# Delta attention, routed experts and a dense layer: five small moves in the first stage

## The chip, the cores and the metric

One core of a Trainium2 chip runs the whole program. The metric is device time in microseconds (us), from three executions of each kernel. Views of the profile come from one further execution, recorded by the hardware profiler.

## The reference

```python
# 1. delta-rule attention, 4 batches x 8 heads, 768 steps, head size 48
k_n = k / (norm(k) + 1e-6)
for t in range(768):
    y[t]  = q[t] @ state
    v_old = k_n[t] @ state
    state = state + beta[t] * outer(k_n[t], v[t] - v_old)
x = y reshaped to 3072 tokens x 384
# 2. router and experts: 8 experts, the best two for each token
logits = x @ w_gate + log1p(exp(x @ w_noise)) * noise
for each token and its best two experts: out += weight * relu(x @ w1[e]) @ w2[e]
# 3. dense layer
h = out @ w_in ; out = (h * clip(h + 3, 0, 6) / 6) @ w_out
```

## The kernel before, in words

The attention works on 24 tiles of 128 tokens (two batches of 64 steps each, all heads). Within a tile the recurrence is written as a triangular system. Its matrix is inverted for four tiles at once, a group, by some 60 VectorE instructions: `inverse_ops(g)`, 1 of 6 groups. They begin with `head`, which transposes the Gram blocks `gd` into `A`, clears `T`, and end with `tail`, which transposes `T` into `Xc` and `Yc`.

The main loop takes two tiles per turn, n = 0, 2, ..., 18. The order of TensorE in a turn is written out by hand: some warming matmuls on zeros (`warm`, L480), `merge1`(n), `ks`(n), the Gram products of tile n+8 (`gram`, L183, into one PSUM tile `gm` that ScalarE evicts at L187 to L205), `merge2`(n), `ks`(n+1), `merge1`(n+1), the router's transposes of tile n-2 (`transposes`, L839), `solve`(n), `merge2`(n+1), transposes of n-1, the router's logits (L852), `update`, `solve`(n+1), `output`, the Gram products of n+9, `update` and `output` of n+1. `merge1` and `solve` of tile n need `Xc` of its group, so a group's inverse must be through when the turn n = 4, 8, 12, 16 or the tail after the loop begins. The tail takes tiles 20 to 23 and starts with `ks`, transposes and `merge1`(20). ScalarE does nearly every eviction of PSUM there.

The instructions of an inverse wait in a list (`pend`) with a cost each; after every step of TensorE `run` lets out as many as the step's time covers. The router works on four tiles at once (`route`, started in the turns n = 4, 8, 12, 16): `scale` (exp and ln on ScalarE, L879 and L880, each with a table load), `noisy` (23 small VectorE instructions, woven one by one between those of the inverse), `count` (sums of the choices, on GpSimd for tiles 0 to 11, on VectorE from tile 12), `rank` (matmuls into a PSUM tile `rk`, read by VectorE at L929 among the woven instructions) and `place` (which queues the scatters of token numbers on GpSimd, `move`). `step` starts the next of these when the last one's woven instructions are out. The tiles `wp`, `tpx`, `lg`, `rk`, `rkt` and half the outputs `y` take turns in two PSUM buffers with the tag `tp`.

In turn n = 18, `reserve` sums the counts of tiles 0 to 15 on TensorE (`rkt`, L818) to find how much of the first expert's block of 512 slots is left over, and shifts that expert's base by it. SyncE issues all loads and stores of the attention in order; the store of an output tile (L834) stands ahead of the next load of queries and keys (`load_qk`, L161).

After the attention come the experts (L1196 and L1219, from 326.6 us of the span), then the dense layer (L1525 and L1557, from 807 us).

Of the kernel before, what the change touches and what calls it, by code (L numbers as in the profile page):

```python
# [16 lines left out]
NH = 8  # L17
CH = 64
P0 = 10
W0 = (3, 6)  # L20
PB = 10
M1_AT = {4: (1, 4, 7), 5: (2, 5), 6: (1, 4)}
W1_AT = {4: (5,), 5: (0,), 6: (0,)}
# [18 lines left out]
EXP = 8  # L42
# [47 lines left out]
def emit_attention(ctx, tc, qk, k, v, beta, const, rt, moe):  # L90
# [156 lines left out]

    big = pr.tile([128, 1024], F32, name="big")
    TT = pr.tile([128, 16, 16], F32, name="TT")

    def blocks(t):
        return t.rearrange("p (s r) -> p s r", s=2)[:, :, 0:512].rearrange("p s (t k) -> p s t k", k=32)[:, :, :, 0:16]

    def inverse_ops(g):
        ops = []
        Af = pr.tile([128, 1056], F32, tag="A", name="A", bufs=1)
        Tf = pr.tile([128, 1056], F32, tag="T", name="T", bufs=1)
        A, T = [t[:, 0:1024].rearrange("p (t i) -> p t i", i=32) for t in (Af, Tf)]
        Ab, Tb = blocks(Af), blocks(Tf)
        scratch = pr.tile([128, 256], F32, tag="tmp", name="tmp", bufs=1)  # L260
# [11 lines left out]

        def head():
            if g:
                nc.gpsimd.memset(Tf[:, 0:1024], 0.0)
            V.transpose(out=A, in_=gd[g].rearrange("p j t -> p t j"))
            V.tensor_copy(out=n2, in_=Af[:, 0:1024:33])
            if g == 0:
                nc.scalar.sqrt(s, n2)
# [228 lines left out]
    def step(drain=False):  # L508
        if drain:
            while stages or micro[0]:  # L510
                while micro[0]:
                    pend.pop(0)[1]()
                if stages:
                    weave(stages.pop(0)() or [])
        elif stages and not micro[0]:
            weave(stages.pop(0)() or [])
            run(0.0)

    def straight(k):
# [94 lines left out]
    for n in range(0, NT - 4, 2):  # L614
        a = n + LA
        four = n % 4 == 0
        pc[0] = a
        if not four and a // 4 + 1 < NG:
            load_beta(a // 4 + 1)
        for i in range(2):  # L620
            live(load_v, n + 4 + i)
            if n + 4 < NT:
                live(load_k, n + 2 + i)
        for i in range(2):
            if n + 2 + i > 3:
                live(v_norm, n + 2 + i)
        if n == NT - 6:
            moe.snapshot(pk, ps2)
            rt.reserve()
        if n:  # L630
            warm(W0[four])
            live(merge1, n)
            live(prep, n)
            live(ks, n)
            live(gram, a)
            live(prep, n + 1)
            live(merge2, n)
            flush(2)
            live(ks, n + 1)
            live(merge1, n + 1)  # L640
            rt.transposes(n - 2, xs.pop(n - 2))
            if n == NT - 6:
                straight(2)
            else:
                step()
            live(solve, n)
            live(merge2, n + 1)
            flush()
            rt.transposes(n - 1, xs.pop(n - 1))
            rt.logits(n - 2)  # L650
        else:
            live(solve, n)
            live(gram, a)
            flush()
        step()
        live(update, n)
        live(solve, n + 1)
        if n:
            rt.logits(n - 1)
            if four:  # L660
                step(True)
                stages += rt.route(n - 4, 4)
                step()
        live(output, n)
        live(load_qk, a + 2)
        if n == NT - 8:
            run(1.0)
            straight(2)
        else:
            step()  # L670
        live(gram, a + 1)
        live(update, n + 1)
        flush(2)
        live(output, n + 1)
        if n == NT - 6:
            while rt.moves:
                rt.moves.pop(0)[1]()
                if not rt.moves:
                    moe.snap_load()
        flush()  # L680
        live(load_qk, a + 3)
        if n != NT - 8:
            step()
        if not four:
            run(0.0, True)
            if n == NT - 10:
                step()
            if n // 4 + 2 < NG:
                pend += inverse_ops(n // 4 + 2)
                run(2.3)  # L690
# [32 lines left out]
    merge2(n + 3)  # L723
    ks(n + 2)
    ks(n + 3)
    stages.pop(0)()
    micros = stages.pop(0)()

# [39 lines left out]
class Router:  # L768
# [87 lines left out]
    def route(self, n, w):  # L856
# [19 lines left out]
        def scale():  # L876
            while self.defer_act:
                self.defer_act.pop(0)()
            nc.scalar.activation(out=e, in_=z, func=ACTF.Exp)  # L879
            nc.scalar.activation(out=l, in_=e, func=ACTF.Ln, bias=1.0)  # L880

        def noisy():
# [35 lines left out]
        def rank():  # L918
            rk = self.ps.tile([128, 4, 128], F32, tag="tp", name="rk", bufs=2)
            out = rk[:, 0, 0:w * EXP]  # L920
            nc.tensor.matmul(out, lhsT=self.ones, rhs=self.base.unsqueeze(1).to_broadcast([128, w, EXP]),
                             start=True, stop=False)
            for j in range(w - 1):
                nc.tensor.matmul(out[:, (j + 1) * EXP:], lhsT=self.ones,
                                 rhs=cnt[:, j].unsqueeze(1).to_broadcast([128, w - 1 - j, EXP]),
                                 start=False, stop=False)
            nc.tensor.matmul(out, lhsT=self.upper, rhs=cnt.rearrange("p j e -> p (j e)"), start=False, stop=True)
            return [
                lambda: V.tensor_tensor(out=pos, in0=out.rearrange("p (j e) -> p j e", e=EXP),  # L929
                                        in1=self.ebase.unsqueeze(1).to_broadcast([128, w, EXP]), op=ALU.add),  # L930
                lambda: V.tensor_tensor(out=oh, in0=oh, in1=pos.unsqueeze(2).to_broadcast([128, w, 2, EXP]),
                                        op=ALU.mult),
                lambda: V.tensor_reduce(out=sf, in_=oh, axis=AX.X, op=ALU.add),
                lambda: V.tensor_copy(out=self.slots[:, n:n + w], in_=sf),
            ]
# [13 lines left out]
        def place():  # L949
            self.moves += [(j, lambda j=j, k=k: move(j, k)) for j in range(n, n + w) for k in range(2)]  # L950

        return scale, noisy, count, rank, place


def overflow_table(tc, rt, kp):
# [123 lines left out]
class Moe1:  # L1079
# [81 lines left out]
    def emit(self, ctx, wd, m2, x_last):  # L1161
# [106 lines left out]
        def tail(f):  # L1268
            if f == 0:
                first[0]()  # L1270
                micro.extend(first[1]())
                rt.transposes(NT - 1, x_last)
                rt.logits(NT - 2)
            elif f == 1:
                some(99)
                first[2]()
                rt.logits(NT - 1)
                final[0]()
            elif f == 2:
                put_pairs(*first[3:])  # L1280
                micro.extend(final[1]())
            elif f == 3:
                some(99)
                final[2]()
            elif f == 4:
                put_pairs(*final[3:])
                rt.total()
                load_ids()
            elif f == 5:
                for q in rt.defer_act + rt.defer_dve:  # L1290
                    q()
                rt.defer_act, rt.defer_dve = [], []
                wd.load()
                self.load(1, 1)
                wd.load()
# [372 lines left out]
```

## Time and profile before

| | us |
|---|---|
| median of 3 executions | 1204.99 |
| lowest and highest | 1200.16, 1214.01 |
| the profiled execution | 1217.92 |
| its span, first to last instruction | 1216.2 |
| TensorE busy in the span | 1145.9 (94%) |
| VectorE, ScalarE, GpSimd busy | 676.5, 510.5, 304.5 |

Times in the views are microseconds from the start of the span. "Idle before" is the time in which an engine stood still ahead of an instruction, with what ended it behind the arrow. The granted clock is TensorE's, as a share of 2.4 GHz.

### The profile page before, as it was taken

What the parts mean: (1) busy time and instruction counts of PE and PEld (TensorE: products, weight loads), DVE (VectorE), ACT (ScalarE), POOL (GpSimd) and SP (SyncE); (2) the same over time, 40 slices, a digit from 0 to 9 for tenths busy, and PEclk for the clock granted to TensorE, in tenths of its full rate; (3) what the DMA queues carried; (4) which work ended last, traced back from release to release, by engine and by line L of the source; (5) the groups of instructions that cost most, each with busy time, mean ns of one, the idle gap of its engine ahead of it and who ended that gap; (6) DMA issues with size and microseconds to landing.
All of it is one profiled execution on the core that took longest, in us unless ns stands there. A gap on an engine that the chain in (4) does not pass through costs nothing. (4 is left out here: it accounts for less than half of the span.)

```text
span 1216.2 us, 25655 instructions
## 1 busy us (share of the span) xinstructions
PE 1145.9 (94%) x10572; PEld 1052.3 (87%) x10587; DVE 676.5 (56%) x1568; ACT 510.5 (42%) x1053; POOL 304.5 (25%) x375
## 2 busy tenths in 40 slices
PE   8888888868789999999999999989999999999998
PEld 5677777757678999999999999978989898999988
DVE  7998677683454858575656644435161524425150
ACT  5667666633542423232333333346151524334240
POOL 4643254564334231414141311124000000000000
PEclk9887797956799999999999999999999999999999
DMA  7652242323216644444453320442102020100000
GB/s 193 144 133 68 67 109 54 80 41 79 94 40 217 229 164 143 151 162 153 126 170 135 126 91 32 145 156 78 51 3 72 7 66 13 49 30 6 22 1 27
DMA packets 56220, 113.35 MB, mean 93 GB/s; under 512 B 9368, under 2 KB 37221, under 8 KB 55334
## 3 DMA queue, kind: packets, MB, share of 16 engines
q1 hardware_dynamic: 47142, 90.32, 25.0%
q0 software_dynamic: 8448, 19.70, 4.9%
q10 hardware_dynamic: 512, 1.67, 0.6%
q8 instruction: 84, 1.38, 0.5%
q14 instruction: 34, 0.28, 0.1%
HBM read 83.74 MB, written 26.08 MB: 90 GB/s over the span
## 5 line engine op out<-in xcount | busy, mean ns | idle before, releaser
L1219 PE MATMUL yp<-w2h,ht 128*128 128x384 f32 x832 | 221.1, 340 | 0.0
L1219 PE MATMUL yp<-w2l,ht 128*128 128x384 f32 x448 | 150.2, 335 | 0.0
L1219 PEld LDWEIGHTS yp<-w2h,ht 128*128 128x128 f32 x832 | 148.4, 188 | 0.3
L1009 POOL DMA_INDIRECT y<-ys,idp x56 | 64.9, 1159 | 301.2 <-DVE ys L1228 222.6
L1196 PE MATMUL hp<-xth,w1h 128*128 128x416 f32 (+2 forms) x384 | 137.1, 357 | 1.2 <-DVE xtl L1138 1.2
L1196 PE MATMUL hp<-xtl,w1h 128*128 128x416 f32 (+2 forms) x384 | 135.9, 354 | 0.0
L1196 PE MATMUL hp<-xth,w1l 128*128 128x416 f32 (+2 forms) x384 | 135.8, 354 | 0.0
L1557 PE MATMUL yp<-woh,gh 128*128 128x384 f32 x384 | 130.4, 340 | 0.0
L1557 PE MATMUL yp<-woh,gl 128*128 128x384 f32 x384 | 129.1, 336 | 0.0
L1557 PE MATMUL yp<-wol,gh 128*128 128x384 f32 x384 | 129.1, 336 | 0.0
L1199 ACT ACTIVATE ht<-hp 128x416 fp32r<-128x416 f32 (+2 forms) x128 | 66.4, 519 | 134.6 <-PE hp L1196 120.3
L1202 DVE SCALAR_TENSOR_TENSOR ht<-hp,ht 128x352 fp32r<-128x352 f32 (+3 forms) x192 | 79.2, 441 | 64.8 <-ACT ht L1199 63.7
L1525 PE MATMUL hp<-xh,wih 128*128 128x512 f32 x288 | 112.8, 392 | 2.6 <-DVE three L1511 2.6
L1525 PE MATMUL hp<-xh,wil 128*128 128x512 f32 x288 | 112.9, 392 | 0.0
L1525 PE MATMUL hp<-xl,wih 128*128 128x512 f32 x288 | 112.7, 391 | 0.0
L1534 DVE TENSOR_TENSOR gl<-r,gh 128x512 fp32r<-128x512 f32 x96 | 66.5, 693 | 79.2 <-ACT gh L1533 79.2
L1528 ACT ACTIVATE r<-hp,three 128x512 f32<-128x512 f32 x96 | 66.2, 690 | 88.9 <-PE hp L1525 81.3
L1530 DVE SCALAR_TENSOR_TENSOR r<-r,hp 128x512 f32<-128x512 f32 x96 | 65.3, 681 | 53.1 <-ACT r L1528 53.1
L1219 PEld LDWEIGHTS yp<-w2l,ht 128*128 128x128 f32 x448 | 84.2, 188 | 0.0
L1196 PEld LDWEIGHTS hp<-xth,w1h 128*128 128x128 f32 x384 | 72.7, 189 | 3.6 <-DVE xtl L1138 1.6
L1564 ACT ACTIVATE os<-yp 128x384 f32<-128x384 f32 x23 | 11.3, 492 | 153.7 <-PE yp L1557 153.7
L1196 PEld LDWEIGHTS hp<-xth,w1l 128*128 128x128 f32 x384 | 72.8, 190 | 2.0
(227 smaller groups left out, 2217.9 us busy)
## 6 DMA issues: line engine op xcount, KB each, us to landing
r<-in_moe_w_dram SPq DMA_DIRECT2D x16, 768.0 KB
r<-in_moe_w_dram SPq DMA_DIRECT2D x21, 512.0 KB
yg<-y SPq DMA_DIRECT2D x24, 384.0 KB
wd_r<-in_moe_w_in_dram SPq DMA_DIRECT2D x6, 1024.0 KB
wd_r<-in_moe_w_out_dram SPq DMA_DIRECT2D x8, 768.0 KB
mq<-in_qk_dram SPq DMA_DIRECT2D x28, 192.0 KB
v<-in_v_dram SPq DMA_DIRECT2D x24, 192.0 KB
xd<-x SPq DMA_DIRECT2D x24, 192.0 KB
```

The costliest lines, as they stand in the source:

```text
L1009: return nc.gpsimd.indirect_dma_start(out=y, out_offset=bass.IndirectOffsetOnAxis(ap=idx, axis=0), in_=src, in_offset=None, bounds_check=y ...
L1196: nc.tensor.matmul(p[:, 0:w], lhsT=a[:, k, fs], rhs=b[:, k, c], start=(i == 0), stop=(i == 3 * KD - 1))
L1199: nc.scalar.activation(out=h[:, c], in_=p[:, 0:w], func=ACTF.Relu)
L1202: nc.vector.scalar_tensor_tensor(out=h[:, rest(lo, hi)], in0=p[:, lo - c.start:hi - c.start], scalar=0.0, in1=h[:, lo:hi].bitcast(F32), op ...
L1219: nc.tensor.matmul(p[0:2 * m if pair else m, 0:DM], lhsT=a, rhs=b[:, f, :], start=f == i == 0, stop=f == FT - 1 and i == len(terms) - 1)
L1525: nc.tensor.matmul(p, lhsT=a[:, k, fs], rhs=b[:, k, :], start=(i == 0), stop=(i == 3 * KD - 1))
L1528: nc.scalar.activation(out=r, in_=p, func=ACTF.Relu, bias=three)
L1530: nc.vector.scalar_tensor_tensor(out=r, in0=r, scalar=6.0, in1=p, op0=ALU.min, op1=ALU.mult)
L1534: nc.vector.tensor_tensor(out=gl[:, f, :], in0=r, in1=gh[:, f, :].bitcast(F32), op=ALU.subtract)
L1557: nc.tensor.matmul(p[:, 0:DM], lhsT=a[:, f, c], rhs=b[:, f, :], start=(i == 0), stop=(i == 3 * FT2 - 1))
L1564: nc.scalar.mul(out=t, in_=p[:, 0:DM], mul=1.0 / 6.0)
```

## The change

Five things are moved or replaced. The ranks are copied from PSUM by ScalarE, and VectorE reads the copy. The router's exp and ln are two stages of their own, so that `step` starts them at different places of the loop; the places of `step` are moved too (after the first `gram` of a turn in place of after the transposes, and only in turns not divisible by four after `load_qk`), and woven router instructions go two by two. The router's transposes of n-2 go in front of the first `gram` of the turn. The sum in `reserve` goes from the head of turn 18 to its end. VectorE clears the diagonal blocks of `T` (half its columns), where GpSimd cleared all of it; `T` is one tile for all groups. Turn 4 has twelve warming matmuls in place of six.

```diff
-W0 = (3, 6)
+W0 = {-1: 3, -2: 6, 4: 12}
...
+    Tf = pr.tile([128, 1056], F32, name="T")
...
         def head():
             if g:
-                nc.gpsimd.memset(Tf[:, 0:1024], 0.0)
+                V.memset(Tb, 0.0)
...
         elif stages and not micro[0]:
-            weave(stages.pop(0)() or [])
+            weave(stages.pop(0)() or [], 2)
...
         if n == NT - 6:
             moe.snapshot(pk, ps2)
-            rt.reserve()
         if n:
-            warm(W0[four])
+            warm(W0.get(n, W0[-(four + 1)]))
             live(merge1, n)
             live(prep, n)
             live(ks, n)
+            rt.transposes(n - 2, xs.pop(n - 2))
             live(gram, a)
             live(prep, n + 1)
+            if n != NT - 6:
+                step()
...
             live(merge1, n + 1)
-            rt.transposes(n - 2, xs.pop(n - 2))
             if n == NT - 6:
                 straight(2)
-            else:
-                step()
...
                 stages += rt.route(n - 4, 4)
-                step()
+                if n == NT - 8:
+                    straight(2)
         live(output, n)
         live(load_qk, a + 2)
         if n == NT - 8:
-            run(1.0)
             straight(2)
-        else:
+        elif not four:
             step()
...
         live(output, n + 1)
         if n == NT - 6:
+            rt.reserve()
             while rt.moves:
...
             nc.scalar.activation(out=e, in_=z, func=ACTF.Exp)
+
+        def log():
             nc.scalar.activation(out=l, in_=e, func=ACTF.Ln, bias=1.0)
...
+            rks = wk.tile([128, w, EXP], F32, tag="rt_rks", name="rt_rks", bufs=1)
+            nc.scalar.copy(out=rks, in_=out.rearrange("p (j e) -> p j e", e=EXP))
             return [
-                lambda: V.tensor_tensor(out=pos, in0=out.rearrange("p (j e) -> p j e", e=EXP),
+                lambda: V.tensor_tensor(out=pos, in0=rks,
```

The tail of the attention and the first expert call the new stage `log` right behind `scale`.

## Rows read from the trace of the kernel before

**Rows 1.** Stretches: length, busy time (instructions) of PE, PEld, DVE, ACT, POOL, clock, DMA, GB/s.

```profile
62.30:81.10 18.80, 17.04 (x481) 15.01 (x481) 18.56 (x41) 14.17 (x36) 6.93 (x8) 1.00 0.45 124
81.10:231.40 150.30, 128.15 (x2906) 112.63 (x2911) 118.12 (x385) 96.89 (x232) 63.40 (x89) 0.82 0.35 80
363.30:806.00 442.70, 438.83 (x2492) 430.59 (x2491) 263.05 (x478) 150.10 (x277) 123.12 (x107) 1.00 0.44 148
```

**Rows 2.** The same view of three stretches behind waits of TensorE.

```profile
109.80:125.80 16.00, 15.96 (x272) 14.42 (x272) 15.89 (x34) 7.99 (x20) 4.91 (x5) 0.50 0.34 75
145.20:154.20 9.00, 9.00 (x152) 8.62 (x152) 5.25 (x40) 5.72 (x12) 0.10 (x1) 0.56 0.01 2
256.10:276.50 20.40, 19.96 (x374) 17.72 (x377) 18.33 (x43) 8.25 (x21) 13.77 (x19) 0.50 0.04 8
```

**Rows 3.** Timeline of TensorE: start, us, line, out<-in, count, idle before and its end.

```profile
84.56 0.87 PE L389 MATMUL mg<-Xc,goff 32*32 32x32 f32 x32 [2.03 <-DVE Xc L364]
...
105.46 1.14 PE L429 MATMUL ks<-us,mq 128*64 128x48 f32 x32
108.44 0.43 PE L183 MATMUL gm<-mq 64*64 64x128 f32 x2 [1.84 <-ACT gd L202]
109.84 3.67 PE L183 MATMUL gm<-mq 64*64 64x128 f32 x30 [0.97 <-DMA mq<-in_qk_dram]
...
114.43 1.95 PE L429 MATMUL ks<-us,mq 128*64 128x48 f32 x32
...
132.31 0.69 PE L389 MATMUL mg<-Xc,goff 32*32 32x32 f32 x32
...
256.13 0.19 PE L818 MATMUL rkt<-rt_acc,ones 128*128 128x8 bf16 x1 [10.80 <-DVE rt_acc L915]
...
282.21 0.69 PE L389 MATMUL mg<-Xc,goff 32*32 32x32 f32 x32
```

**Rows 4.** Waits from 62 to 282: engine, line, waited for, total, times, longest.

```profile
PE lg L852 <- DVE rt_pos L929: 7.2, 2, 4.1
...
PE gm L183 <- ACT gd L202: 4.5, 4, 1.8
```

**Rows 5.** Timeline of ScalarE, turn 4 and turn 8.

```profile
98.45 0.48 ACT L841 COPY rt_xt<-tpx 128x384 f32<-128x384 f32 x1
...
102.60 1.28 ACT L880 ACT_TABLE_LOAD   x1
103.89 0.23 ACT L880 ACTIVATE rt_t<-rt_t 128x32 f32<-128x32 f32 x1
104.03 0.46 ACT L150 COPY x<-y 128x384 f32<-128x384 f32 x1
...
136.71 0.76 ACT L152 ACTIVATE Xc<-mg 32x256 f32<-32x256 f32 x2 [1.17 <-PE mg L408]
```

**Rows 6.** Timeline of VectorE: start, inverse of group 2, inverse of group 5.

```profile
1.00 0.48 DVE L121 MEMSET mg<- 128x512 f32 x1 [1.00 <-PEq L1652]
...
49.59 0.69 DVE L297 TENSOR_TENSOR sm<-sm 128x32 f32<-128x32 f32 x1
...
102.61 0.18 DVE L885 TENSOR_SCALAR rt_t<-rt_t 128x32 f32<-128x32 f32 x1 [1.93 <-ACT rt_t L879]
...
123.51 1.93 DVE L364 STREAM_TRANSPOSE Xc<-T 128x1024 f32<-128x1024 f32 x1
...
233.93 1.98 DVE L276 STREAM_TRANSPOSE A<-gd 128x1024 f32<-128x1024 f32 x1 [1.86 <-ACT gd L202]
...
244.28 0.20 DVE L308 COPY T<-sm 128x32 f32<-128x32 f32 x1 [3.70 <-POOL T L275]
...
254.53 0.19 DVE L901 TENSOR_TENSOR rt_cnt<-rt_oh 128x32 bf16<-128x32 f32 x1
...
265.94 0.19 DVE L929 TENSOR_TENSOR rt_pos<-rk,ebase 128x32 f32<-128x32 f32 x1 [1.62 <-PE rk L927]
...
276.14 1.99 DVE L364 STREAM_TRANSPOSE Xc<-T 128x1024 f32<-128x1024 f32 x1
```

More of the change, by code (lines that the diff above doesn't have):

```diff
@@ L256, in inverse_ops @@
         Af = pr.tile([128, 1056], F32, tag="A", name="A", bufs=1)
-        Tf = pr.tile([128, 1056], F32, tag="T", name="T", bufs=1)
         A, T = [t[:, 0:1024].rearrange("p (t i) -> p t i", i=32) for t in (Af, Tf)]
@@ L725, in emit_attention @@
     ks(n + 3)
+    stages.pop(0)()
     stages.pop(0)()
@@ L950, in place @@
             self.moves += [(j, lambda j=j, k=k: move(j, k)) for j in range(n, n + w) for k in range(2)]
-        return scale, noisy, count, rank, place
+        return scale, log, noisy, count, rank, place
 def overflow_table(tc, rt, kp):
@@ L1270, in tail @@
                 first[0]()
-                micro.extend(first[1]())
+                first[1]()
+                micro.extend(first[2]())
                 rt.transposes(NT - 1, x_last)
@@ L1275, in tail @@
                 some(99)
-                first[2]()
+                first[3]()
                 rt.logits(NT - 1)
                 final[0]()
+                final[1]()
             elif f == 2:
-                put_pairs(*first[3:])
-                micro.extend(final[1]())
+                put_pairs(*first[4:])
+                micro.extend(final[2]())
             elif f == 3:
                 some(99)
-                final[2]()
+                final[3]()
             elif f == 4:
-                put_pairs(*final[3:])
+                put_pairs(*final[4:])
                 rt.total()
```

## The prediction

> **What bounds the kernel now.** I read the stretches first. From 363 us on TensorE is busy for 438.8 of 442.7 us at a clock of 1.00 [rows 1]; nothing that the change touches shortens that, it only begins earlier or later. All the time to be had lies before. A turn of the loop in which nothing goes wrong is there to see: turn 2, from 62.3 to 81.1, 18.8 us at full clock, with TensorE busy for 17.0 of it. The six turns after it, 4 to 14, take 150.3 us where six such turns would take 112.8, at a mean clock of 0.82 [rows 1].
>
> Then the timeline of TensorE, for what comes ahead of the slow stretches: waits of two to eleven microseconds, each with a stretch at half clock, 1.2 GHz, behind it [rows 2, 3]. Twice the logits wait for VectorE to read a rank out of PSUM, 4.1 and 3.1 us [rows 4]; in turn 6 the Gram products wait 1.84 us for ScalarE's evictions and 0.97 for a load; at the head of turn 18 the count sum waits 10.8 us for VectorE [rows 3]. What half clock costs is read from one group at either level: `ks` takes 1.14 us at 105 and 1.95 at 114 [rows 3], so a stretch at half clock would be 1 - 1.14/1.95 = 0.42 of itself shorter.
>
> Last the chain of VectorE, the engine that could become the bound. The inverse of group 5 goes from `head` at 233.93 to the end of `Xc` at 278.1, and TensorE wants that result at 282.2 [rows 3, 6]. It is only 4 us ahead.
>
> **The change part by part.** I went through the order in which the loop lets out its instructions, by its costs and credits, and laid it on the times of the trace.
>
> *Rank copied by ScalarE.* The buffer `rk` has tag `tp`, so the logits two tiles later need it free. Before, VectorE reads it only when the inverse's list comes to it; now a ScalarE copy, queued right behind the matmuls, frees it. Such a copy doesn't stand in the trace; a 32-wide ScalarE instruction takes 0.23 us and a 384-wide copy from PSUM 0.48 [rows 5]; I take 0.3, nearer to the first. It hides in the ScalarE time spent waiting for TensorE. The two waits, 7.2 us, go; what is late next at the logits is their own `rt_xt` copy, which is queued earlier.
>
> *Exp and ln in different turns.* Now the pair stands in turns 4, 8 and 12 ahead of the copy of an output, which starts at 104.03 when ln is through [rows 5]. Behind it are the evictions that turn 6's Gram products wait for, and, through the store in SyncE's order, the load that they wait for next. The new exp goes behind those evictions, at the end of the turn; ln stands two microseconds of TensorE work later, ahead of the eviction of `merge2`. So the 1.84 and 0.97 go, with those of turns 10 and 14: four waits of this kind are 4.5 us in all, which leaves 2.7 for the three besides turn 6 [rows 3, 4], and I count 0.9 for each. In their place comes a wait for ScalarE: each of the two costs 1.28 + 0.23 = 1.51 us, the transposes' copy moved ahead 0.48, against 1.17 us that ScalarE stood idle at that point [rows 5]: 1.51 + 1.51 + 0.48 - 1.17 = 2.3 us for turns 6, 10 and 14 each, spread over `solve` and `merge2`. Behind ScalarE's ln are queued the evictions of `merge2`(n), `ks`(n+1) and `merge1`(n+1), and TensorE waits for these.
>
> The trace has a table load of 1.28 us for exp and again for ln [rows 5], with the two side by side; apart there are two as well, so I add none. The Trainium skill (ScalarE: Activation LUTs, section "Rules for kernel authors") says to finish all of one table set before switching, and to budget about 2.7 us for a switch. By that figure each of the two places would hold 1.4 us more, and the sum below would be 3 x 2 x 1.4 = 8.4 us worse; the trace's 1.28 speaks against it (and for the 1283 ns of the same page's section on the load's cost), and decides.
>
> *Transposes in front of the Gram products.* The same three matmuls; they fill what is left of the Gram's wait. Nothing, with the copy's 0.48 already counted.
>
> *Count sum later.* At the end of turn 18 its counts are long there, and its three VectorE instructions stand among the last of inverse 5 as before among the middle ones. What is late next is the rank of tiles 12 to 15, which needs the same choices. VectorE has those at 254.7 [rows 6], less 3.2 us by the next paragraph: 251.5. TensorE would come to the rank at 245.3 + 0.58 x 9.8 = 251.0, from the 9.8 us between the count sum and the rank's reader at half clock [rows 3, 6]. A wait of half a microsecond.
>
> *VectorE clears `T`.* Half of 1024 columns is 512, and the memset of that size at the start takes 0.48 us [rows 6]; blocks of 16 may make it up to twice that. It removes VectorE's wait behind GpSimd's queue, 3.70 us in group 5 [rows 6] and about as much in group 4. Net 3.2 earlier in group 5.
>
> *Twelve warming matmuls in turn 4.* They lie in the 2.03 us wait for `Xc` [rows 3]. Nought to minus 3 us, if the clock then holds up; I take 0.
>
> **The sum, by stages.** Turns 4 and 6: -2.8 waits, -6.7 half clock (16.0 x 0.42 [rows 2]), +2.3 = **-7.2**. The inverse of group 2 must be through by then: its `Xc` ends at 125.4, less the 1.93 us that VectorE waited for exp, plus two memsets, 124.5 [rows 6]; TensorE came for it at 132.3 [rows 3], so up to 7.8 us fit. Turns 8 and 10: -4.1, -3.8 (9.0 x 0.42 [rows 2]), -0.9, +2.3 = **-6.5**. Turns 12 and 14, with a stretch at half clock like that one, counted the same: -3.1, -3.8, -0.9, +2.3 = **-5.5**. Turn 16 to `merge1`(20): TensorE alone would gain 10.8 + 20.4 x 0.42 = 19.4 [rows 2, 3], but VectorE doesn't: 278.1 less 3.7 for GpSimd, less 1.6 for the rank [rows 6], plus 0.5, is 273.3 against 282.2, **-8.9**. After that TensorE stands idle for some 9 us ahead of `merge1`(20) and does the next 4 us, which were at full clock, at half: +2. Three ranks in the tail with the extra copy: +1. Together -25.1.
>
> The profiled execution took 1217.9, 12.9 above the median of 1205.0. The waits follow from the order of the instructions, so all runs should have them; I take the 25.1 from the median: **1180 us**.
>
> **The rivals.** *VectorE becomes the bound of every group.* Its small instructions take 0.69 us in place of 0.19 while GpSimd works beside them [rows 6], and the scatters of the ranks now meet other parts of the inverse. Three more microseconds in each of four groups are 12, of which the stages have some 5 to spare (0.6 in turns 4 and 6; the second and third gain 3 or more from VectorE's own waits): +7, 1187. For it: the -8.9 already ends at VectorE. Against it: in turns 8 and 12 VectorE waits for ScalarE, not the reverse.
>
> *ScalarE's ln brings the half clock back.* The new 2.3 us is as long as the 2.03 at 84.56 that had half clock behind it [rows 3]. In three turns, at 9.0 x 0.42 = 3.8 each, +11.4: 1191. Against it: it comes in two pieces.
>
> *Slower.* The table loads now stand in two turns out of two, no longer in one. If each brings a wait long enough that the clock doesn't come back before the next, a turn takes 18.8/0.58 = 32.4 us. With k of six turns so, the loop takes 112.8 + 13.6k for 150.3 before; with -8.9 and +3 behind it the kernel is slower from k = 4, where it is 1216, and 1243 at six. Against it: turn 2 runs at full clock with ScalarE busy for 14.2 of 18.8 [rows 1], and 3 more leave room.
>
> *The change doesn't do what it says*, because the reader of the rank wasn't what held the buffer, and the counts are as late as before: then only the first stage's 7.2 remains: 1198.
>
> **How the numbers follow.** Forecast 0.50, with a range of its own of 1172 to 1187; VectorE the bound 0.22; half clock after ln 0.15; slower 0.07; no effect 0.06. The range of 8 in 10 goes from 1168 (the warming matmuls and the 3 us gained, and waits of the profiled run) to 1197. A run of this kernel tells a difference of about 1%, 12 us: the first two cases and most of the third are faster, 0.78; the rest of the third and the last within 1%, 0.15; slower 0.07.
>
> **What would show it.** In the profile after: no `lg` wait on `rt_pos`; no wait at L818; `gm` waiting less than a microsecond; ScalarE's two table loads some 5 us apart; `T` copied without a wait on GpSimd; a new idle of TensorE ahead of `merge1`(20), ended by `Xc`; the start of the experts near 302 in place of 326.6. It is wrong if new waits of 2 us with half clock behind them stand in turns 6, 10 and 14, or if the inverse of a group takes longer than 40 us.

## The result and the profile after

The changed kernel takes 1189.33 us (median of 7 runs, 1186.67 to 1192.59) against 1207.14 us for the kernel before on the same chip (7 runs, 1195.00 to 1214.01): ratio 0.9866, interval 0.9834 to 0.9899, 17.8 us faster. A second measurement on another chip gave 0.9828 (0.9773 to 0.9882). Ratios leave out disturbed executions, so they can stand a little off the ratio of the medians. The forecast was 1180 in a range of 1168 to 1197.

The profiled execution of after took 1189.55 us (span 1187.8), within a quarter of a microsecond of its median. That of before had taken 1217.9, some 11 above its own: between the two profiles lie 28.4 us, between the medians 17.8. This gap matters below.

The stretches first, the turns 4, 6, 8, 10, 12 and 14, then turn 16 to `merge1`(20), then from there to the first product of the experts (columns as in [rows 1]):

```profile
81.15:100.32 19.17, 18.69 (x492) 15.77 (x491) 16.59 (x81) 14.52 (x37) 5.92 (x8) 1.00 0.37 98
100.32:123.97 23.65, 21.27 (x484) 19.01 (x482) 19.83 (x43) 17.36 (x41) 7.35 (x8) 0.78 0.35 97
123.97:142.16 18.19, 17.71 (x492) 15.46 (x489) 14.43 (x68) 14.50 (x38) 8.37 (x15) 1.00 0.40 107
142.16:167.18 25.02, 22.81 (x484) 20.39 (x482) 24.19 (x62) 17.53 (x42) 14.32 (x18) 0.73 0.41 86
167.18:189.05 21.87, 20.75 (x493) 18.36 (x490) 18.45 (x82) 14.66 (x38) 11.10 (x19) 0.84 0.39 93
189.05:214.53 25.48, 21.55 (x489) 19.19 (x487) 22.19 (x48) 19.14 (x46) 13.66 (x18) 0.80 0.30 65
214.53:258.76 44.23, 35.88 (x908) 31.53 (x909) 40.78 (x141) 25.07 (x62) 32.46 (x51) 0.83 0.34 61
258.76:297.92 39.16, 32.43 (x718) 29.10 (x718) 19.93 (x63) 17.96 (x39) 10.88 (x11) 0.67 0.43 123
```

The six turns take 133.4 us in place of 150.3 [rows 1]. Two of them, 4 and 8, now run at full clock, about as fast as turn 2. Turns 6, 10 and 14 do not, each at 0.73 to 0.80, and neither does turn 12, at 0.84. Taken one by one, turns 4 to 14 took 23.0, 26.8, 25.7, 21.0, 29.7 and 24.1 us before: 4, 6, 8 and 12 became 3 to 8 us shorter, but 10 and 14 became longer, by 4.0 and 1.4. From the first product of the experts to the end it is 1187.8 - 297.9 = 889.9 us, before 1216.2 - 326.6 = 889.6. Everything that was won stands ahead of the experts, as forecast.

What turns 6, 10 and 14 have in common stands in TensorE's timeline (columns as in [rows 3]; `issue` in place of an engine means that the profile shows nothing that TensorE waited for):

```profile
81.15 2.76 PE L480 MATMUL wp<-wz 128*128 128x512 bf16 x11
83.84 0.69 PE L389 MATMUL mg<-Xc,goff 32*32 32x32 f32 x32
...
109.11 0.69 PE L389 MATMUL mg<-Xc,goff 32*32 32x32 f32 x32 [1.99 <-ACT Xc L152]
...
151.04 0.69 PE L389 MATMUL mg<-Xc,goff 32*32 32x32 f32 x32 [1.99 <-ACT Xc L152]
...
177.89 0.38 PE L408 MATMUL mg<-y,Yc 32*32 32x32 f32 x12 [0.92 <-issue]
...
197.93 0.69 PE L389 MATMUL mg<-Xc,goff 32*32 32x32 f32 x32 [1.99 <-ACT Xc L152]
...
250.99 0.18 PE L819 MATMUL rkt<-rt_acc,ones 128*128 128x8 bf16 x1
...
258.76 1.06 PE L389 MATMUL mg<-Xc,goff 32*32 32x32 f32 x32 [5.12 <-DVE Xc L364]
```

The long waits of [rows 3] and [rows 4] are gone: `merge1`(4) finds its `Xc` ready behind the warming matmuls, the Gram products don't wait in turn 6, no logits wait for a rank, and the count sum (now L819) doesn't wait. Three new waits of 1.99 us stand at `merge1`(n+1) in turns 6, 10 and 14, and one of 5.12 at `merge1`(20). Behind each of the three, TensorE ran mostly at the lower level, 1.2 GHz: the granted clock was 0.57 from 109.8 to 121.8, 0.51 from 152.5 to 166.0 and 0.59 from 199.5 to 212.0. Turn 12 has a stop of another kind: `merge2` stands still for 0.92 us ahead of its last twelve matmuls, with nothing to wait for, and the clock is 1.00 before it and 0.67 and 0.71 in the two stretches behind (177.9 to 182 and 182 to 189).

What `merge1` waited for is ScalarE (timeline of ScalarE, turn 6):

```profile
103.39 1.28 ACT L880 ACT_TABLE_LOAD   x1
104.68 0.23 ACT L880 ACTIVATE rt_t<-rt_ls 128x32 f32<-128x32 f32 x1
...
105.99 0.48 ACT L842 COPY rt_xt<-tpx 128x384 f32<-128x384 f32 x1
...
106.89 1.28 ACT L883 ACT_TABLE_LOAD   x1
108.18 0.23 ACT L883 ACTIVATE rt_t<-rt_t 128x32 f32<-128x32 f32 x1
108.32 0.74 ACT L152 ACTIVATE Xc<-mg 32x256 f32<-32x256 f32 x2
```

ScalarE is busy from 103.39 to 109.06 without a gap: exp with its load, four evictions, the router's copy, ln with its load. The last line is the eviction of `merge2` that `merge1` needs. Ln is directly ahead of it and exp some 4 us ahead, and both, 1.51 us each, delay it.

### The profile page after: what moved, and what is told of

It is laid out like the page before. It is cut to its first block, busy times and chain, and to the rows that moved or that the text cites. A ratio compares the mean times of both kernels' runs of the same rounds, so it can differ in the third digit from the quotient of the medians.

```text
span 1187.8 us, 25674 instructions
## 1 busy us (share of the span) xinstructions
PE 1139.6 (96%) x10578; PEld 1047.3 (88%) x10593; DVE 677.7 (57%) x1573; ACT 509.8 (43%) x1060; POOL 302.5 (25%) x370
## 5 line engine op out<-in xcount | busy, mean ns | idle before, releaser
L1571 ACT ACTIVATE os<-yp 128x384 f32<-128x384 f32 x23 | 11.3, 491 | 152.8 <-PE yp L1564 152.8
```

Source lines behind the costliest of these rows:

```text
L1571: nc.scalar.mul(out=t, in_=p[:, 0:DM], mul=1.0 / 6.0)
```

## The experiments

Twelve kernels ran, four on each of three chips. A ratio is always to the kernel before on the same chip, whose median was 1209.5 for the first four kernels, 1219.2 for the next four and 1211.3 for the last four. Times across chips are therefore compared by ratio. The changed kernel ran on the third of these chips (experiment 9), but not on the second.

**1. Exp one place earlier.** The stage with exp goes ahead of the eviction of the output in turns 4, 8 and 12, and ln takes the place that exp had, behind the evictions of the next turn's first Gram products.

```diff
                 if n == NT - 8:
                     straight(2)
+                else:
+                    step()
         live(output, n)
```

> The changed kernel with exp one place earlier: in turns 4, 8 and 12 it starts ahead of the copy of an output, where exp and ln stood before the change; ln moves up to the end of those turns, and nothing of the router stands ahead of the eviction of merge2 in turns 6, 10 and 14. Theory A (ln in ScalarE's order holds merge1 for 1.99 us in these three turns, and half clock follows: 12, 14 and 11 us of it): the three waits go, each pair of turns gets 5 to 7 us shorter until VectorE's inverse is the bound, and the kernel takes about 1172 us (1168 to 1179). Theory B (the wait comes from the transposes' copy moved ahead, or another engine is late next): 1186 to 1190, as the changed kernel's 1189.

1181.5 us, ratio 0.9764 (0.9720 to 0.9807). Stretches (turns 6 and 14), TensorE's timeline, and ScalarE's for turn 6:

```profile
102.27:120.22 17.95, 16.94 (x484) 14.90 (x482) 17.54 (x41) 15.62 (x39) 7.47 (x8) 1.00 0.45 136
...
183.68:203.66 19.98, 17.44 (x489) 15.33 (x487) 19.50 (x46) 17.34 (x43) 13.61 (x16) 1.00 0.38 87
```

```profile
109.49 0.69 PE L389 MATMUL mg<-Xc,goff 32*32 32x32 f32 x32 [0.42 <-ACT Xc L152]
...
190.90 0.69 PE L389 MATMUL mg<-Xc,goff 32*32 32x32 f32 x32 [0.43 <-ACT Xc L152]
...
245.93 0.69 PE L389 MATMUL mg<-Xc,goff 32*32 32x32 f32 x32 [2.88 <-DVE Xc L364]
...
267.17 0.24 PE L1159 MATMUL tpi<-ident,idf 4*128 4x4 f32 x1 [6.58 <-DMA idf<-ids]
```

```profile
99.24 1.28 ACT L882 ACT_TABLE_LOAD   x1
...
105.33 1.28 ACT L885 ACT_TABLE_LOAD   x1
...
108.69 0.74 ACT L152 ACTIVATE Xc<-mg 32x256 f32<-32x256 f32 x2
```

The 1.99 us waits shrink to 0.42 and 0.43 or vanish, and turns 6 and 14 run at full clock, 5.7 and 5.5 us shorter; turn 10, at 0.92, is 3.5 shorter. Contrary to the expectation, ln has not left the queue in front of `merge2`'s eviction: it runs at 105.33, three microseconds ahead. What left is exp, which now runs at 99.24, ahead of the output's copy; its 1.51 us are what the wait lost (1.99 - 0.42 = 1.57). So exp and ln together in that queue, and the half clock behind the wait, are the cause of the three slow turns. Turn 12 isn't helped (23.8 us at 0.78). `merge1`(20) begins 12.8 us earlier (245.9 for 258.8), the experts only 5.4 (292.5 for 297.9): 6.58 us go to a new wait, for the load of the snapshot's indices (token numbers of the first expert's block, which are loaded back and transposed ahead of the gathers of its rows). The time lies just above theory A's range.

**2. Six warming matmuls in turn 4.**

```diff
-W0 = {-1: 3, -2: 6, 4: 12}
+W0 = {-1: 3, -2: 6}
```

> The changed kernel with six warming matmuls in turn 4 in place of twelve. Theory A (the extra six take the place of a wait of 2 us, so the clock stays up through turn 4, where before 7 us were at half): the wait of 1.3 to 2 us at merge1(4) and the half clock are back, +3.8 us, 1193. Theory B (the clock holds without them, or VectorE is late next): 1189.

1190.8, ratio 0.9855 (0.9812 to 0.9898): nothing that can be told from the changed kernel. In the profile a wait for VectorE stands at `merge1`(4), and turn 4 is no longer at full clock throughout. Below are TensorE's line here, the same line of experiment 6, which has the twelve, and the end of VectorE's inverse in the changed kernel:

```profile
82.28 1.06 PE L389 MATMUL mg<-Xc,goff 32*32 32x32 f32 x32 [5.21 <-DVE Xc L364]
```

```profile
83.24 0.69 PE L389 MATMUL mg<-Xc,goff 32*32 32x32 f32 x32 [4.61 <-DVE Xc L364]
```

```profile
78.11 1.97 DVE L364 STREAM_TRANSPOSE Xc<-T 128x1024 f32<-128x1024 f32 x1
```

The six missing matmuls are at most 1.3 us of that wait (2.76 against 1.47 us of warming). In this execution TensorE came to turn 4 earlier than in the changed kernel (its warming matmuls begin at 75.6 for 81.2); in that of experiment 6 it came as early (75.9) and waited all the same, with twelve. In the changed kernel's profile `Xc` is complete at 80.1, before the first warming matmul, so that there was no wait to cover. From `merge1`(4) to the warming matmuls of turn 6 it takes 100.96 - 82.28 = 18.7 us here, 18.0 in experiment 6 and 100.32 - 83.84 = 16.5 in the changed kernel, at clocks of 0.86, 0.91 and 1.00. What the twelve are worth is not shown. Turn 14 is shorter here, as it waits only 0.59 us for ScalarE in this execution and then runs at 1.00.

**3. The rank read from PSUM again.**

```diff
-            rks = wk.tile([128, w, EXP], F32, tag="rt_rks", name="rt_rks", bufs=1)
-            nc.scalar.copy(out=rks, in_=out.rearrange("p (j e) -> p j e", e=EXP))
...
-                lambda: V.tensor_tensor(out=pos, in0=rks,
+                lambda: V.tensor_tensor(out=pos, in0=out.rearrange("p (j e) -> p j e", e=EXP),
```

> The changed kernel without the ScalarE copy: VectorE reads the ranks in PSUM again. Theory A, the prediction's (the copy is what frees the buffer): waits of 3 to 4 us at the logits in turns 8 and 12 with half clock behind them, +14, 1203. Theory B (the new places of step put the rank where VectorE reads it a few microseconds later, so the copy hardly matters): a wait of up to 1 us, 1189 to 1191.

1190.2, ratio 0.9849 (0.9814 to 0.9884): theory B. Waits of TensorE, 62 to 282:

```profile
PE lg L853 <- DVE rt_pos L932: 1.0, 1, 1.0
```

1.0 us in place of the 7.2 of [rows 4], without the copy: VectorE reads the rank in time but for that. The copy is not what took the wait away; what is left for it are the places at which the steps now stand.

**4. The router's transposes back behind merge1.**

```diff
-            rt.transposes(n - 2, xs.pop(n - 2))
             live(gram, a)
...
             live(merge1, n + 1)
+            rt.transposes(n - 2, xs.pop(n - 2))
```

> The changed kernel with the router's transposes of n-2 behind merge1(n+1), as before. Theory A (ln is what holds merge1 in turns 6, 10 and 14; the transposes' copy ahead of it adds 0.4 us): that wait falls from 1.99 to about 1.6 us, the Gram products wait 0.3 to 0.6 us instead, and the time stays within 3 us of 1189. Theory B (the copy is the cause): the wait and the half clock behind it go, 1175 or less.

1187.1, ratio 0.9846 (0.9801 to 0.9891): no worse. Timeline of TensorE at the third of three such waits, all of 1.61 us, and the stretch behind it:

```profile
198.31 0.69 PE L389 MATMUL mg<-Xc,goff 32*32 32x32 f32 x32 [1.61 <-ACT Xc L152]
```

```profile
199.00:212.60 13.60, 11.59 (x297) 9.83 (x297) 11.81 (x33) 11.36 (x30) 8.39 (x13) 1.00 0.14 44
```

Moving the copy of 0.48 out of ScalarE's full stretch shortens the wait by 0.38. Behind the third wait TensorE kept full clock. The Gram products wait for ScalarE's evictions for 2.5 us in all here, at most 0.6 each, and for 0.2 in the changed kernel. So the transposes in front exchange a wait at the Gram for one at `merge1`, and neither is large enough to show in the time.

**5. Ln with exp again.** Both stand where exp stands in experiment 1; the stage of ln is empty.

```diff
+                else:
+                    step()
...
             nc.scalar.activation(out=e, in_=z, func=ACTF.Exp)
+            nc.scalar.activation(out=l, in_=e, func=ACTF.Ln, bias=1.0)

         def log():
-            nc.scalar.activation(out=l, in_=e, func=ACTF.Ln, bias=1.0)
+            pass
```

> The changed kernel with one part undone: exp and ln of the router's noise stand together again, ahead of the eviction of the output in turns 4, 8 and 12; the stage that would hold ln is empty. All the rest is as changed (rank copies, transposes in front, later count sum, VectorE's clears, warming matmuls). Theory A (taking the two apart is worth only what it takes off the Gram's wait, and it loses about that at merge1): the three 1.99 us waits of merge1 for ScalarE go, with their half clock, and the wait of the Gram products for ScalarE's evictions comes back, some 1 to 2 us in turns 6, 10 and 14, with a stretch at half clock behind it; time 1185 to 1193, within 4 us of the changed kernel. Theory B (taking them apart is what the change lives on): the Gram waits and the half clock come back in full, 1196 to 1204, and the three turns are each 3 us longer than in the changed kernel.

1198.8 on the slowest of the three chips, ratio 0.9846 (0.9774 to 0.9919): by ratio the same as the changed kernel, theory A, though the microseconds, for another chip, fall in theory B's range. Waits of TensorE in the whole execution:

```profile
PE gm L183 <- DMA mq<-in_qk_dram: 6.7, 6, 2.1
...
PE gm L183 <- ACT gd L202: 1.5, 2, 1.4
```

`merge1` has no wait for ScalarE's `Xc`. The Gram products wait instead, and mostly not for ScalarE but for the load of q and k: the output's copy stands behind the pair (2 x 1.51 = 3.0 us), its store behind the copy, and the load behind the store in SyncE's order. As it was done, taking the two apart exchanged one wait for another. The single execution of the profile also holds 12.4 us of waits for issue, the most of all, so its turns (23.6 us for turn 10, 28.6 for turn 14) don't price the exchange.

**6. The count sum at the head of turn 18 again.**

```diff
             moe.snapshot(pk, ps2)
+            rt.reserve()
...
         if n == NT - 6:
-            rt.reserve()
             while rt.moves:
```

> The changed kernel with one part undone: the count sum stands again at the head of turn 18, where it stood before. Theory A (VectorE's inverse of group 5 sets the end of this stretch, as the prediction has it): the wait at the count sum comes back, 3 to 11 us, but merge1(20) waits for VectorE anyway, so that its wait of 5.12 shrinks by as much; the time rises by 0 to 5 us for the half clock, 1189 to 1194, and merge1(20) begins within 3 us of 258.8. Theory B (the wait at the count sum was worth itself): merge1(20) begins 8 or more us later and the time is 1197 to 1203.

1203.2, ratio 0.9869 (0.9791 to 0.9948): by ratio the same as the changed kernel. Waits and timeline of TensorE:

```profile
PE rkt L819 <- DVE rt_acc L916: 8.2, 2, 7.4
```

```profile
265.04 0.69 PE L389 MATMUL mg<-Xc,goff 32*32 32x32 f32 x32
```

The largest wait of the kernel before is back, 7.4 us, and the one ahead of `merge1`(20) is gone. TensorE waits early or late, as theory A has it, but here VectorE is no longer what sets the end: its `Xc` is complete at 260.1, 5 us before `merge1`(20) begins. `merge1`(20) begins 6 us later than in the first profile of the changed kernel, which misses theory A's sign of 3 us, but on this chip the place of the count sum shows no difference: from turn 16 to `merge1`(20) it takes 49.9 us here and 50.9 and 49.8 in experiments 5 and 7, which have the sum late (and 3.0 and 3.6 us of waits for issue in that stretch).

**7. GpSimd clears the blocks again.**

```diff
-                V.memset(Tb, 0.0)
+                nc.gpsimd.memset(Tf[:, 0:1024], 0.0)
```

> The changed kernel with one part undone: GpSimd clears the inverse's blocks again, and not VectorE. Theory A (VectorE sets the end of the last group alone): the copy into the blocks waits again for GpSimd, 3 to 4 us in groups whose inverse has GpSimd's queue ahead of it; in groups 1 to 4 TensorE doesn't see it, in group 5 merge1(20) begins 2 to 4 us later; time 1190 to 1194. Theory B (VectorE's chain is what every group waits for): merge1 of each group begins 3 us or more later and the time is 1198 to 1205. Theory C (nothing waits for it): 1187 to 1190, and merge1(20) begins where it does in the changed kernel.

1207.4 (10 runs), ratio 0.9937 (0.9902 to 0.9972): the only part whose single undoing cost time that can be told, some 0.7 to 1.1% by ratio to the changed kernel on other chips, and 0.7 and 0.4% over experiments 5 and 6 on this one. It fits none of the three theories as they were put. The wait that the memset should bring back is hardly there (waits of VectorE, 60 to 310):

```profile
DVE T L308 <- POOL T L275: 0.4, 1, 0.4
```

0.4 us, in group 4, and none in group 5, where [rows 6] has 3.70. The new places of the steps alone don't explain that: experiment 10 has them and GpSimd's clears, and waits 3.70 us in group 5.

What the clears do to VectorE stands in the first steps of group 1: GpSimd's masks (L245) and VectorE's small instructions, in this kernel and then in the changed one.

```profile
47.77 8.61 POOL L245 TENSOR_SCALAR_AFFINE_SELECT mq<-mq 64x512 f32<-64x512 f32 x12
...
55.75 0.67 DVE L300 TENSOR_TENSOR sm<-sm 128x32 f32<-128x32 f32 x1
56.45 0.18 DVE L301 TENSOR_SCALAR sm<-sm 128x32 f32<-128x32 f32 x1
```

```profile
44.06 7.11 POOL L245 TENSOR_SCALAR_AFFINE_SELECT mq<-mq 64x512 f32<-64x512 f32 x10
...
51.24 0.19 DVE L297 TENSOR_TENSOR sm<-sm 128x32 f32<-128x32 f32 x1
```

GpSimd's memset has to wait until VectorE has read `T` for the last time, and the masks queued behind it come later. While they run, most of VectorE's small instructions take 0.5 to 0.7 us; behind them, from 56.38 here and from 51.17 in the changed kernel, 0.15 to 0.35. From `head` to the copy into `T` group 1 takes 11.3 to 12.3 us in the four profiles in which GpSimd clears and 7.5 to 9.5 in the ten in which VectorE does; to the end of `Xc` 39.1 to 40.3 and 32.6 to 37.8. At `merge1`(4) TensorE waits 0.90 us for that here.

That is less than the ratio says, and the profiled execution can't show the rest: at 1202.7 us it is the fastest of the ten. It also has pauses in turn 16, with no engine or transfer to wait for (timeline of TensorE; the same pattern goes on to 238.6):

```profile
233.45 0.26 PE L451 MATMUL sd<-us,kbd 128*48 128x48 f32 x2 [0.47 <-issue]
```

These don't come from the clears. Experiment 5, with VectorE's, has them in the same place: 3.0 us of them for 3.6, and 20.2 us for turn 16 as against 20.3. The part's price is measured, and its mechanism is shown in part only.

**8. The kernel before, once more** (unchanged, for its profile).

> The kernel before itself, for a second profile. If its profiled execution of 1217.9 us holds waits that its other executions don't have, this one takes 1200 to 1214 us and its turns 4 to 14, or what stands behind merge1(20), are shorter by the difference; if the waits are set by the order of the instructions, the turns have the same lengths within 1 us and the difference stands behind merge1(20).

1222.1, on a chip where its median was 1219.2. Waits of TensorE:

```profile
PE rkt L818 <- DVE rt_acc L915: 10.7, 1, 10.7
PE lg L852 <- DVE rt_pos L929: 7.6, 2, 4.1
```

These two waits are those of [rows 3] and [rows 4] within half a microsecond, so they follow from the order of the instructions. The Gram products' are not: 2.2 us for ScalarE and 3.1 for the load, where the first profile has 4.5 and 1.7. The turns are not the same within 1 us: turn 6 takes 134.25 - 104.18 = 30.1 us for 26.8. Neither reading holds as it was put: the longest waits are the kernel's, the shorter ones and the lengths of the turns are not.

**9. The changed kernel, once more.**

> The changed kernel itself, on the chip on which the next three run. If its time is set by the order of its instructions alone, it takes 1187 to 1193 again and its experts begin within 3 us of 297.9. If the stretches in which TensorE waits for the issue of its own instructions (3.2 us before the experts in its first profile, 12.4 and 10.2 in the two single undoings on another chip) differ from run to run, the experts begin later by the same sum and its half clock, up to 305 to 310, and the time is 1195 to 1205.

1191.5, ratio 0.9828 (0.9773 to 0.9882). The same three waits of 1.99 or 2.00, 5.96 ahead of `merge1`(20), experts at 300.1, waits for issue 6.0 us for 3.2: the first reading.

**10. The order of the steps alone.** The changed kernel without the rank copies, the early transposes, the later count sum, VectorE's clears and the twelve matmuls: the edits of experiments 2, 3, 4, 6 and 7 together.

```diff
-W0 = {-1: 3, -2: 6, 4: 12}
+W0 = {-1: 3, -2: 6}
...
-                V.memset(Tb, 0.0)
+                nc.gpsimd.memset(Tf[:, 0:1024], 0.0)
...
+            rt.reserve()
...
-            rt.transposes(n - 2, xs.pop(n - 2))
             live(gram, a)
...
```

> Of the change only the order of the router's steps is kept: ln in a stage of its own, and the new places of all stages, two micro-operations at a time. Taken out are the rank copies, the transposes in front, the later count sum, VectorE's clears and the twelve warming matmuls. Theory A (the new places carry the gain, since each other part undone alone moved the time by less than 1%): within 5 us of the changed kernel on the same chip, the logits wait less than 1.5 us for rt_pos, and the count sum waits 5 to 8 us but merge1(20) no longer waits for VectorE. Theory B (the other parts cover for one another, and carry more than half of the gain together): 9 us or more above the changed kernel, with the waits of the logits for rt_pos back to 3 us or more and the Gram products waiting 4 us for ScalarE.

1198.6, ratio 0.9897 (0.9848 to 0.9946): 12.7 us under the kernel before and 7.1 above the changed kernel (experiment 9, same chip), between the two theories. Waits of TensorE, 60 to 310:

```profile
PE rkt L819 <- DVE rt_acc L918: 10.1, 1, 10.1
PE mg L389 <- DVE Xc L364: 7.1, 1, 7.1
PE mg L389 <- ACT Xc L152: 4.8, 3, 1.6
PE tpx L840 <- DVE rt_pos L932: 3.2, 2, 2.4
```

Of the 19.9 us between the two kernels on this chip the order alone brings 12.7, some two thirds. The five others bring 7.1 together; the four runs of each kernel don't overlap (1196.8 to 1200.6, 1185.9 to 1193.5). That the five cover for one another isn't shown by that: the clears alone cost as much by ratio (experiment 7, 0.9937). With all five out, the transposes that share the rank's buffer wait 3.2 us for it, the count sum 10.1, and `merge1`(4) 7.1: TensorE comes to turn 4 some 4 us earlier than in experiment 9 (76.1 for 80.5) and `Xc` is complete 2.7 us later (84.5 for 81.9).

**11 and 12. A better version.** Experiment 1, with the snapshot's index behind the last merge; then the same with the transposes of experiment 4.

```diff
     solve(n + 1)
-    moe.snap_index()
...
     merge2(n + 3)
+    moe.snap_index()
```

> The kernel with exp ahead of the output, and the transpose of the snapshot's indices put behind the last merge, some 10 us of TensorE work later. Theory A (the 6.6 us that TensorE waited for the load of the indices is what kept 4 of the 12.8 us from the end): the wait is under 1 us, the experts begin at 286 to 290 in place of 292.5, time 1175 to 1180. Theory B (what sets the start of the experts is the gathered rows, so that a later gather makes the transposes of the rows wait instead): tp waits 3 us or more for xg, the experts begin at 292 or later, time 1181 to 1186.

> As the kernel with the snapshot's index later, and the router's transposes back behind merge1 as in the kernel before. Theory A (ScalarE's queue ahead of merge1 is still what TensorE waits for, and the transposes' copy of 0.48 stands in it): merge1's waits for ScalarE, 0.42 and 0.43, go, and the time is 1 to 3 us under that kernel's, 1173 to 1179. Theory B (with exp ahead ScalarE has room there): no difference beyond 1 us, or up to 3 us more since the three transposes no longer fill TensorE's wait for the load of q and k (0.63 and 1.61 us).

1183.1, ratio 0.9777 (0.9719 to 0.9834), and 1180.3, ratio 0.9747 (0.9697 to 0.9796; 1178.7 to 1181.7 in four runs). Timeline of TensorE in the first, then in the second:

```profile
252.21 1.06 PE L389 MATMUL mg<-Xc,goff 32*32 32x32 f32 x32 [3.81 <-DVE Xc L364]
...
271.35 0.22 PE L1159 MATMUL tpi<-ident,idf 4*128 4x4 f32 x1
```

```profile
251.53 1.06 PE L389 MATMUL mg<-Xc,goff 32*32 32x32 f32 x32 [5.55 <-DVE Xc L364]
...
269.15 0.22 PE L1159 MATMUL tpi<-ident,idf 4*128 4x4 f32 x1
...
288.04 0.79 PE L1203 MATMUL hp<-xth,w1h 128*128 128x512 f32 x1 [1.16 <-DVE xtl L1145]
```

The wait of 6.58 is gone, and ahead of the experts no row waits for the gathers instead, which is theory A of experiment 11, though its time is in theory B's range. From `merge1`(20) to the experts the second takes 36.5 us where experiment 1 took 46.5. That the index's place alone gained time isn't shown, since experiment 1's ratio is within the interval of 11: `merge1`(20) came 6 us later there. Turn 10 took 27.8 us at a clock of 0.63 in that execution, behind a wait of 2.03 us of its Gram products for the load of q and k, which experiment 1 has in two pieces (0.63 and 1.61). The last kernel is 11.2 us faster than the changed one on the same chip (whose fastest of four runs took 1185.9), and 31 faster than the one before. In it no `merge1` waits for ScalarE's `Xc`, and turns 4 to 10 all run at 1.00, in 19.2, 18.4, 18.1 and 18.7 us. Turns 12 and 14 do not: 25.8 us at 0.80 and 23.5 at 0.85, behind 1.46 us for VectorE's `Xc` at `merge1`(12) and 1.99 for issue. That the waits for ScalarE go with the transposes back is theory A of experiment 12; whether it is faster by that is within what these runs leave uncertain.

## Why the prediction was right or wrong

It had the sign, the place and the range right, but in three of the six turns not the mechanism: the sign that it had given for being wrong, new waits of 2 us with half clock behind them in turns 6, 10 and 14, is what the profile shows, and turns 10 and 14 became longer. That the time still lies in the range is in part luck, as gains that the sum did not have made up for it. (Its other sign, an inverse of over 40 us, could not tell the two apart: by its own reading group 5 takes 278.1 - 233.9 = 44.2 us in the kernel before.) Stage by stage, with the first warming matmul of each turn as the boundary in both profiles:

| stage | forecast | profile before | profile after | difference |
|---|---|---|---|---|
| turns 4 and 6 | -7.2 | 49.8 | 42.8 | -7.0 |
| turns 8 and 10 | -6.5 | 46.7 | 43.2 | -3.5 |
| turns 12 and 14 | -5.5 | 53.8 | 47.4 | -6.5 |
| turn 16 to `merge1`(20) | -8.9 | 50.8 | 44.2 | -6.6 |
| from there to the experts | +3.0 | 44.4 | 39.2 | -5.2 |
| sum | -25.1 | | | -28.8 |

The second profiles of the two kernels (experiments 8 and 9, on two chips) give -7.7, -6.3, -2.1, -8.1 and -3.7, so a stage is known to some 4 us at best.

**What put the number 9 us off is the last step of the sum**, "I take the 25.1 from the median". The sum was read from an execution 10.8 us above the median of its runs (12.9 above that of the three known then), and against that execution it is right within 4 us (1217.9 - 25.1 = 1192.8, measured 1189.6), with errors of both signs in the stages. The reason given, that the waits follow from the order, holds for the longest waits (experiment 8), not for what stands behind them: on one chip the kernel before took 1204.4 us at a mean clock of 0.952 and 1217.1 at 0.941. How much of the half clock a run meets varies, and the profile, at 0.945, seems to have caught much of it. The forecast was 1180; taken from the profiled execution it would have been 1193.

**Ln brings half clock back.** This rival, with 0.15, is what happened in turns 6, 10 and 14, in a kernel that is faster all the same, and its 1191 is nearer to the measured 1189 than the forecast's 1180. The forecast found ScalarE's 2.3 us and even the eviction of `merge2` as the one that waits, but spread it over two places and charged no half clock. It came as one wait, 1.99 us, with the two table loads 3.5 us apart and not some 5. The rival priced the half clock at 3.8 us a turn; taking the wait away shortened the turns by 5.7, 3.5 and 5.5 us, 14.7 in all; with the waits themselves taken off (3 x 1.99 less the 0.85 that is left) that is 3.2 a turn. Experiment 1 shows it with the same instructions, one place earlier: exp's 1.51 us out of that queue shorten the wait by 1.57. (Turn 10 still had its wait for the load there, so 3.2 is not the half clock of these waits alone.)

**Turn 4**, where the sum had only the warming matmuls, as nought of a range to -3, is 3.8 us shorter and at 1.00. Its wait of 2.03 us went because VectorE is through earlier: `Xc` is complete at 80.1 in place of 84.5, with TensorE at the same point (81.2 and 81.1). That goes with VectorE's clears: with GpSimd's, group 1's inverse is longer again (experiment 7); the forecast credited them in groups 4 and 5 alone. This gain is why turns 4 and 6 fit the forecast although turn 6 kept its half clock: two errors that cancel.

**The rank copy** was credited with the 7.2 us of waits. They went, but the copy alone doesn't do it: without it 1.0 us is left (experiment 3). They went because the steps moved: in experiment 10, with the order alone, no logits wait for a rank. The copy may be worth something where the places don't suffice, at most the 3.2 us of experiment 10, where the transposes are the ones to wait.

**Exp and ln apart.** The Gram's waits for ScalarE went, as forecast, and a wait of about that size took their place; as a part it is worth nothing that can be told where it was put (experiment 5) and some 8 to 12 us one place earlier (experiment 1, by ratio to the two measurements of the changed kernel). There are two loads of 1.28 us each, as in the trace of before. The budget of some 2.7 us that the Trainium skill gives for a switch (ScalarE: Activation LUTs, section "Rules for kernel authors") does not show here. By the same page's section "What ACT_TABLE_LOAD costs" that budget is some 1283 ns of load and some 1380 ns of drain, so the two figures that the prediction set against each other agree on the load. Of the drain this trace shows nothing: the instruction ahead of the load ends 0.02 us before it (103.37 and 103.39), and exp begins 0.01 us behind it.

**Count sum and VectorE's clears.** The new idle ahead of `merge1`(20), ended by `Xc`, stands there with 5.12 us where some 9 were forecast, so VectorE is the bound of that stretch in the changed kernel, and the count sum's wait was, as forecast, worth little by itself (experiment 6): with the count sum back, TensorE waits earlier and by the time of `merge1`(20) VectorE is through. The clears were to take 3.2 us off group 5. Undoing them brings no wait back there (experiment 7), yet costs 0.7 to 1.1%, of which the longer inverse of group 1 is the part that is seen.

**From `merge1`(20) to the experts** +3 was forecast and -5.2 came. TensorE did run at a low clock there (0.67), but it had done so before as well (0.70), and in the profile of before 6.6 us of waits stand in this stretch (2.4 for issue, 2.4 for `y`, 1.8 for `Xc`) and 1.4 of the same kinds in that of after. The forecast had counted the work of this stretch and not its waits.

## What to carry to other kernels

Before a sum is taken from the median of the runs, see where the profiled execution stands among them, and against which of the two each term holds. A slow instruction that is moved out of one engine's queue goes in front of something else; find the first matmul that needs what is queued behind it, and charge the whole wait to that one with the half clock behind it. Compare each turn with itself before adding turns up: a pair of turns that gained 3.5 us here hid one that lost 4.0. And undo parts together as well as singly, on one chip and beside the changed kernel: only so can it be told whether five parts that cost 7 us at once cover for one another, or whether the one that costs something alone is all of it, which these runs leave open.

## What the hardware showed that was not expected

The waits of 1.99 to 2.00 us at `merge1` in the two profiles of the changed kernel were followed by half clock; of those of 1.61 us five of six were (three in experiment 10, granted clock 0.64 to 0.66, and two of three in experiment 4, 0.76 and 0.67), and one was not. Behind the waits of 0.42, 0.43 and 0.59 us of experiments 1 and 2 it kept 1.00.

VectorE's small instructions (128 x 32) take 0.67 to 0.69 us in place of 0.19 while GpSimd runs its masks, and are back at 0.19 at the first that starts when the masks end (51.24 for 51.17 in the changed kernel, 56.45 for 56.38 in experiment 7). So a memset that only made other GpSimd work come later lengthened the first steps of VectorE's inverse by 2 to 5 us, with no wait between the two engines (experiment 7).

TensorE pauses for the issue of its own matmuls, in experiments 5 and 7 mostly about 0.45 us after every two or three of them, and for up to 2.6 us at once (experiment 8). Between 60 and 310 us these pauses come to 9.6 and 8.7 us in the two profiles of before, 3.2 and 6.0 in those of the changed kernel and 1.8 to 12.4 in the variants, with no engine named as the cause. One of them keeps its place: in turn 12 of the changed kernel and of every variant the same `merge2` stops near its end, for 0.5 to 2.0 us, and in all but one of these profiles (experiment 5's) turn 12 is below full clock, at 0.78 to 0.92. No change here was aimed at these pauses.
